# A 2D DFT with a cosine layer behind it: four small moves of work beside a full TensorE

## Chip, cores and metric

The kernel runs on one core of a Trainium2 chip. The metric is the device time of one execution in microseconds (us), lower is better. Every number below is the median of several executions, is read from one profiled execution, or is worked out from such numbers. All executions in this study are recorded as fast (an execution in a slower state would not have been compared).

TensorE multiplies matrices. In this kernel its products go to PSUM, and what the engines read otherwise lies in SBUF (two on-chip memories).

The profile splits TensorE into PE (the matmul passes) and PEld (the weight loads, which overlap the passes: in the kernel before 1932.9 and 1649.2 us of busy time in a span of 1982.3). DVE is VectorE, ACT is ScalarE, POOL is GpSimd, SP is SyncE, which here only issues DMA. A trailing q (SPq) marks an engine's sequencer, which issues its instructions. The granted clock is the share of full speed that TensorE was given (1.00 is full). L276 is line 276 of the kernel; `pB<-G,WT` is an instruction that writes tile pB from tiles G and WT. Nearly every operation goes through a one-line helper, so a line number names the kind of operation, and the tiles tell which one it is.

## The reference, cut to what matters

```python
# x: [8, 3008, 256] float32; w_in: [256, 2048]; w_out: [2048, 256]
X = np.fft.fft(np.fft.fft(x, axis=1), axis=2).real    # over the sequence, then over the channels
X = X.reshape(8 * 3008, 256)
h = X @ w_in
g = h * np.cos(h)
out = g @ w_out                                       # [24064, 256]
```

## The kernel before

The channel DFT is folded into `w_in` at the start (`fold_sin`, `fold_cos` give Ws and Wc). The sequence DFT of a batch uses its symmetries: rows of `x` are added and subtracted ("folds", on GpSimd after the first batch), and the folded rows are multiplied by sine and cosine matrices. Some rows are needed in reversed order; GpSimd fetches these with indirect DMA ("gathers"). Channel 128 is not covered by the folded weights and is computed for all batches at once, early ("ext" in the code).

The rest is 376 equal steps. Eight steps make one tile of 256 columns and its mirror image, so there are 47 tiles. A step makes two hidden blocks (`H`), takes the cosine on ScalarE, multiplies on VectorE, forms four sums on GpSimd (`sum_1` to `sum_4`), and multiplies into four accumulators in PSUM, `pA` to `pD`. Only one set of the four exists, so the next tile's products wait until the old ones have been read. This is how work is placed: each function has a time in units of the planned step `T` = 4.8 us, and the program order of each engine follows from these times.

```python
        for dt, fn in (
            (-1.9, ext), (0.0, mm_P), (0.9, dbl), (2.17, mm_Q), (3.55, h_minus),
            ...
            (T + 0.9, r_minus), (T + 1.5, sin_plus), (T + 2.2, g_plus), (T + 2.21, sin_minus),
            (T + 2.9, g_minus), (T + 2.91, sum_1), (T + 3.6, sum_3), (T + 4.4, sum_2),
            (2 * T + 0.3, sum_4), (2 * T + 0.87, mm_X1), (2 * T + 3.04, mm_X2),
        ):
            at(t + dt, lambda fn=fn, i=i: fn(i))
```

At the end of a tile its accumulators are combined. Five operations read them: a ScalarE copy of half of pA and four VectorE adds, the last of which is `comb_3`:

```python
    def comb_3(q):
        T = tiles[q]
        vtt(T.v, T.v, T.acc[3], ALU.add)           # VectorE; acc[3] is pD
    ...
            turns = ((T + 1.2, comb_3), (2 * T + 1.0, turn_u), (3 * T + 1.0, turn_v))
        for dt, fn in ((1.45, comb_copy), (4.2, comb_1), (T + 1.0, comb_2), (T + 1.1, comb_22)) + turns:
```

The DFT of channel 128 reads it with rows on partitions (`MC,xe 128*8` in the timelines below). Before, it was loaded with batches on partitions and then turned through DRAM:

```python
    def turn_ext():
        rows, xs = state["rows"], state["xs"]
        for g in range(2):
            spin(out=xe_dr[g], in_=rows[g][:, 0:768])              # to DRAM
            spin(out=xr_dr[g], in_=rows[g][:, 247::-1])
        for g in range(2):
            spin(out=xs[:, g, :, 0:4], in_=...)                    # back, in runs of a few rows
            ...                                                    # (three more loads for each g)
```

The loads and gathers of batch `b` start 8 steps ahead of the point `s0` where its period of 47 steps begins, one gather a step, and the folds start one step ahead of `s0`:

```python
        l0 = s0 - (8 if b > 1 else 1.2)
        ...
                at((l0 + n) * T + 1.3, lambda b=b, n=n: gather_x(b, state["L"], n))
        f0 = max(7, s0 - 1)
        f1 = s0 + 38
```

## Time and profile before

| | before |
|---|---|
| median, lowest and highest of 3 runs | 1984.32, 1982.59 to 1985.54 us |
| span of the profiled run | 1982.3 us |
| PE busy | 1932.9 us (98%) |
| other engines busy | 72 to 73% each |

The head of the page, the packet count and the chain of work that ended last, of the kernel before:

```profile
PE 1932.9 (98%) x8858; PEld 1649.2 (83%) x8858; DVE 1425.2 (72%) x2386; ACT 1454.8 (73%) x2807; POOL 1418.9 (72%) x1947
...
DMA packets 283624, 65.85 MB, mean 33 GB/s; under 512 B 264570, under 2 KB 275458, under 8 KB 283474
...
PE 84%; DVE 5%; POOL 4%; ACT 3%; issue 2%; SPq 1%; DMA 1%; DVEq 0%; POOLq 0%
```

TensorE bounds this kernel: the other engines matter only where they make it wait. The table by windows of the kernel before says where it was idle; its columns are the window, its length, and the busy time (with instruction count) of each engine, then the granted TensorE clock, the DMA share and GB/s:

```profile
0.00:50.00 50.00, 39.84 (x121) 21.93 (x122) 26.25 (x59) 14.17 (x27) 35.77 (x55) 0.97 1.07 255
50.00:100.00 50.00, 49.34 (x223) 40.91 (x222) 36.27 (x60) 37.12 (x71) 45.09 (x73) 1.00 1.29 36
100.00:150.00 50.00, 25.56 (x126) 19.29 (x125) 17.56 (x29) 18.04 (x36) 18.99 (x31) 0.76 0.36 22
150.00:400.00 250.00, 247.99 (x1138) 213.20 (x1139) 185.21 (x312) 188.86 (x365) 191.46 (x259) 1.00 0.14 31
```

Half of the window from 100 to 150 us is idle. The timeline of PE and that of SP, kernel before (start, duration, instruction, and in brackets the idle time before it and what ended it):

```profile
106.01 0.59 PE L276 MATMUL pD<-G,w 128*128 128x256 f32 x2
130.26 3.73 PE L276 MATMUL H<-MC,xe 128*8 128x190 f32 x28 [23.66 <-POOL xe L285]
```

```profile
67.20 0.42 SPq L162 DMA_DIRECT2D xe_dr<-x  x1
...
77.01 39.34 SPq L162 DMA_DIRECT2D xs<-xe_dr  x3
...
123.53 1.04 SPq L162 DMA_DIRECT2D xs<-xr_dr  x1
```

This is "the hole": TensorE stood still for 23.66 us because the round trip of channel 128 through DRAM, whose first store was issued at 67.20 us, had not come back. The three loads at 77.01 us alone held SyncE's sequencer for 39.34 us.

The table of waits of the kernel before (engine and line, what it waited for: total us, how often, longest):

```profile
PEld H L276 <- POOL xe L285: 24.4, 2, 24.1
...
PE H L276 <- POOL xe L285: 23.7, 1, 23.7
...
PEld pB L276 <- POOL G L285: 18.5, 49, 1.0
...
PE pB L276 <- POOL G L285: 2.3, 8, 0.6
```

The hole stands in it twice, once for the weight load and once for the matmul. The third and fourth lines are one wait too, that of the product into pB for a GpSimd sum.

### The profile page before, as it was taken

How to read it: one execution, taken by the hardware profiler on the slowest of the kernel's cores; microseconds unless marked ns; L12 is line 12 of the kernel's file. 1: busy time of each engine (PE TensorE's matmuls, PEld its weight loads, DVE VectorE, ACT ScalarE, POOL GpSimd, SP SyncE). 2: the span in 40 equal slices, each digit the busy share in tenths (PEclk: the TensorE clock that was granted, in tenths of full speed). 3: DMA queues.
4: the chain of work that ended last, by engine and by line, in shares of the span. 5: the costliest groups of instructions: out<-in, count | busy, mean ns of one | idle time of the engine just before them, and what ended most of it. 6: DMA issues, size and time to landing. Idle time of an engine off the chain costs nothing.

```text
span 1982.3 us, 28384 instructions
## 1 busy us (share of the span) xinstructions
PE 1932.9 (98%) x8858; PEld 1649.2 (83%) x8858; DVE 1425.2 (72%) x2386; ACT 1454.8 (73%) x2807; POOL 1418.9 (72%) x1947
## 2 busy tenths in 40 slices
PE   7959999999999999999999999999999999999998
PEld 4838888888888888888888888888888888887887
DVE  5737777777777777777767777777776777777777
ACT  2737777777777777777777777777777777777776
POOL 7837768777687767877777776877768786555664
PEclk9979999999999999999999999999999999999999
DMA  9930111102110021100210002111021110100101
GB/s 258 36 22 20 51 32 31 25 12 52 39 22 20 12 60 44 20 11 14 65 45 13 14 13 66 35 19 24 9 67 28 21 21 15 17 11 12 22 11 22
DMA packets 283624, 65.85 MB, mean 33 GB/s; under 512 B 264570, under 2 KB 275458, under 8 KB 283474
## 3 DMA queue, kind: packets, MB, share of 16 engines
q1 hardware_dynamic: 276386, 51.06, 16.2%
q0 software_dynamic: 4912, 12.73, 2.4%
q8 instruction: 70, 1.15, 0.3%
q14 instruction: 80, 0.66, 0.1%
q10 hardware_dynamic: 2176, 0.26, 0.1%
HBM read 39.13 MB, written 24.82 MB: 32 GB/s over the span
## 4 chain that ended last, share of the span: by engine, by line
PE 84%; DVE 5%; POOL 4%; ACT 3%; issue 2%; SPq 1%; DMA 1%; DVEq 0%; POOLq 0%
PE H L276 33%; PE pB L276 14%; PE pC L276 14%; PE pD L276 14%; PE pA L276 7%; POOL G L285 2%; DVE G L790 2%; ACT G L288 1%; SPq L162 1%; POOL xl L152 1%; DVE G L282 1%; POOL e L341 1%; DVE v L282 1%; DVE M L282 1%; ACT E L288 1%
## 5 line engine op out<-in xcount | busy, mean ns | idle before, releaser
L285 POOL TENSOR_TENSOR G<-G 128x256 f32<-128x256 f32 x1500 | 1079.0, 730 | 504.5 <-DVE G L790 416.3
L790 DVE SCALAR_TENSOR_TENSOR G<-H,G 128x512 f32<-128x512 f32 x376 | 256.9, 683 | 289.5 <-ACT G L288 289.0
L282 DVE TENSOR_TENSOR G<-H,G 128x512 f32<-128x512 f32 x376 | 259.8, 691 | 220.9 <-ACT G L288 217.8
L288 ACT ACTIVATE G<-H 128x512 int32<-128x512 f32 x376 | 224.5, 597 | 235.4 <-DVE G L282 234.0
L276 PE MATMUL pC<-G,WT 128*128 128x256 f32 x1504 | 387.4, 379 | 2.7 <-DVE u L282 2.2
L276 PE MATMUL H<-Rr,Wc 128*128 128x256 f32 x1504 | 387.6, 380 | 1.6 <-ACT H L288 0.9
L276 PE MATMUL H<-Ir,Ws 127*128 127x256 f32 x1504 | 387.4, 379 | 0.7 <-ACT E L288 0.7
L288 ACT ACTIVATE E<-H 128x512 f32<-128x512 f32 x376 | 224.2, 596 | 219.0 <-PE H L276 213.9
L288 ACT ACTIVATE H<-Rb,wex 128x256 f32<-128x256 f32 x752 | 360.3, 479 | 26.3 <-DVE G L790 10.3
L276 PEld LDWEIGHTS H<-Rr,Wc 128*128 128x128 f32 x1504 | 283.4, 190 | 50.8 <-ACT H L288 5.4
L276 PEld LDWEIGHTS pC<-G,WT 128*128 128x128 f32 x1504 | 283.8, 189 | 46.8 <-PE H L276 6.8
L276 PEld LDWEIGHTS H<-Ir,Ws 127*128 127x128 f32 x1504 | 282.5, 189 | 44.8 <-ACT E L288 5.9
L288 ACT ACTIVATE G<-G,halfpi 128x512 f32<-128x512 f32 x376 | 269.6, 717 | 1.5 <-DVE G L282 1.5
L282 DVE TENSOR_TENSOR M<-G,M 128x512 f32<-128x512 f32 x376 | 257.7, 685 | 0.0
L282 DVE TENSOR_TENSOR G<-E,H 128x512 f32<-128x512 f32 x376 | 255.1, 678 | 3.1 <-PE H L276 2.7
L790 DVE SCALAR_TENSOR_TENSOR G<-G,M 128x512 f32<-128x512 f32 x376 | 254.1, 676 | 0.4 <-ACT M L288 0.3
L288 ACT ACTIVATE M<-M,halfpi 128x512 f32<-128x512 f32 x376 | 246.6, 656 | 0.4 <-DVE M L282 0.3
L276 PE MATMUL pB<-G,WT 128*128 128x256 f32 x752 | 228.6, 386 | 2.8 <-POOL G L285 2.3
L276 PE MATMUL pB<-G,w 128*128 128x256 f32 x752 | 223.7, 379 | 0.6 <-DVE u L282 0.6
L288 ACT ACTIVATE M<-G 128x512 int32<-128x512 f32 x376 | 224.1, 596 | 0.0
L276 PE MATMUL pA<-G,w 128*128 128x256 f32 x752 | 223.8, 379 | 0.1
L276 PE MATMUL pD<-G,w 128*128 128x256 f32 x752 | 223.7, 379 | 0.0
(150 smaller groups left out, 1855.7 us busy)
## 6 DMA issues: line engine op xcount, KB each, us to landing
out_dram<-ot SPq DMA_DIRECT2D x496, 32.0 KB
xl<-in_x_dram SPq DMA_DIRECT2D x32, 256.0 KB
out_dram<-ot SPq DMA_DIRECT2D x256, 2.0 KB
xl<-in_x_dram SPq DMA_DIRECT2D x31, 128.0 KB
Rb<-r SPq DMA_DIRECT2D x10, 376.0 KB
w<-in_moe_w_in_dram SPq DMA_DIRECT2D x4, 512.0 KB
w<-in_moe_w_out_dram SPq DMA_DIRECT2D x1, 2048.0 KB
MC<-dft_mats SPq DMA_DIRECT2D x2, 942.0 KB
```

Source lines behind the costliest of these rows:

```text
L152: nc.gpsimd.indirect_dma_start(out=L[j][:, part[0] * ND : part[1] * ND], out_offset=None, in_=xflat, in_offset=bass.IndirectOffsetOnAxis(a ...
L162: pin(nc.sync.dma_start(**kw))
L276: nc.tensor.matmul(out_, lhsT=lhsT, rhs=rhs, start=start, stop=stop, skip_group_check=True)
L282: pin(nc.vector.tensor_tensor(out=o, in0=a, in1=b, op=op))
L285: pin(nc.gpsimd.tensor_tensor(out=o, in0=a, in1=b, op=op))
L288: pin(nc.scalar.activation(out=o, in_=i, func=func, **kw))
L341: pin(eng.tensor_tensor(out=o, in0=a, in1=b, op=f))
L790: nc.vector.scalar_tensor_tensor(out=o, in0=h, scalar=TWO_PI, in1=c, op0=ALU.mult, op1=ALU.mult)
```

## The change

It has four parts.

1. **The turn.** Channel 128 is turned by TensorE: slices of the loaded rows are the weights, a small 0/1/-1 matrix (`pick`) is streamed, and the product is the turned and folded channel. The store and loads through DRAM go, and so does the GpSimd fold.
2. **The gathers.** Two adjacent ones are merged, and the loads start 10 steps ahead of `s0`, the folds at `s0`, so that gathers and folds of a batch no longer fall into the same steps.
3. **The copy.** ScalarE copies pD, the last quarter of the product sums, to SBUF. VectorE's add of it moves by nearly a step; the transposes move by a step.
4. **The start.** The last two folds of `w_in` come earlier (one ahead of I's first DFT, the other into another PSUM bank), and the first step's elementwise work goes ahead of an unfold.

The diff, cut to its core (constants, the index table and the first load's bookkeeping are left out):

```diff
+    def open_ext():
+        ps = state["turned"] = bank("H")
+        pin(nc.vector.memset(ps[:, 0:128], 0.0))
+        rows = state["rows"]
+        pin(nc.gpsimd.tensor_copy(out=rows[:, 1024:1148], in_=rows[:, 247::-2]))
     def turn_ext():
-        ... (four stores to DRAM, eight loads back)
+        rows, ps = state["rows"], state["turned"]
+        even, both, less = (pick[0:32, a:z] for a, z in ((32, 40), (32, 48), (48, 56)))
+        d, m = rows[:, 1024:1148], rows[:, 505:761:2]
+        for lhsT, o, rhs in (
+            (rows[:, 0:512:4], C0, both),
+            (rows[:, 2:512:4], C2, both),
+            ... (eight more)
+        ):
+            mm(ps[0 : lhsT.shape[1], o * 16 : o * 16 + rhs.shape[1]], lhsT, rhs, False)
     def fold_ext():
-        ... (six GpSimd operations)
+        xe = spool.tile([128, 8, 2, NB], FP, tag="xe", bufs=1, name="xe")
+        act(xe.rearrange("p m k b -> p (m k b)"), state["turned"][:, 0:128])
...
-    at(-T, turn_ext)
-    e0 = 12 * T
-    at(e0 + 1.35, fold_ext)
+    e0 = 10 * T
+    at(e0 - 2 * T + 2.905, open_ext)
+    at(e0 - 2 * T + 4.75, turn_ext)
+    at(e0 - T + 1.46, fold_ext)
...
+    def comb_copy3(q):
+        T = tiles[q]
+        T.p3 = spool.tile([128, 512], FP, tag="p3", bufs=1, name="p3")
+        act(T.p3, T.acc[3])
     def comb_3(q):
-        vtt(T.v, T.v, T.acc[3], ALU.add)
+        vtt(T.v, T.v, T.p3, ALU.add)
-            turns = ((T + 1.2, comb_3), (2 * T + 1.0, turn_u), (3 * T + 1.0, turn_v))
+            turns = (
+                (T + 2.3, comb_copy3),
+                (2 * T + 1.0, comb_3),
+                (3 * T + 1.0, turn_u),
+                (4 * T + 1.0, turn_v),
+            )
...
+            if j == 2 or b < NB - 1:
+                yield j, (3, 6), n                 # gathers: one of (3,6) for (3,4) and (5,6)
...
-        l0 = s0 - (8 if b > 1 else 1.2)
+        l0 = s0 - (10 if b > 1 else 1.2)
-        f0 = max(7, s0 - 1)
-        f1 = s0 + 38
+        f0 = max(7, s0)
+        f1 = s0 + (36 if b > 1 else 38)
...
+    fold_cos(3)                                    # now ahead of I_even.first
...
+    ahead = {r_minus: T + 0.3, sin_plus: T + 0.85, sin_minus: T + 0.86,
+             g_plus: T + 0.92, g_minus: T + 0.93, sum_1: T + 0.94}
+            if i == 0:
+                dt = ahead.get(fn, dt)
-        (0.95, lambda: fold_sin(3, "pD")),
+        (0.95, lambda: fold_sin(3)),
-        (3.0, lambda: state.update(wc3=fold_mms(3, 0, "pA"))),
-        (4.81, lambda: act(Wc[:, 1536:2048], state.pop("wc3"))),
```

More of the change, by code (lines that the diff above doesn't have):

```diff
@@ L85, in _pick_consts @@
 def _pick_consts():
-    m = np.zeros((128, 32), np.float32)
+    m = np.zeros((128, 56), np.float32)
     m[np.arange(128), np.arange(128) % 32] = 1.0
+    q = np.arange(32)
+    c = 32 + q % 16 // 2
+    m[q, c] = 1.0
+    m[q, c + 8] = np.where(q // 16 == q % 2, 1.0, -1.0)
+    m[q, c + 16] = -1.0
     return m
@@ L95, in _row_consts @@
     for base in (HALF, SEQ):
-        cols += [base - _row_of(m) for m in (C0, C2, M1, X1)]
-    cols.append(SEQ - _row_of(D1))
+        cols += [base - _row_of(m) for m in (C2, M1, X1)]
+    cols += [SEQ - _row_of(m) for m in (C0, D1)]
     return np.clip(np.stack(cols, axis=1), 0, SEQ - 1).astype(np.uint32)
@@ L144, with gather_x @@
     xflat = x.rearrange("b s d -> (b s) d")
-    ix = cpool.tile([128, 11], U32, tag="ix")
+    ix = cpool.tile([128, 10], U32, tag="ix")
     nc.sync.dma_start(out=ix, in_=IX_dr.ap())
-    def gather_x(b, L, n):
-        j, part = GATHERS[n]
+    def gather_x(b, L, g):
+        j, part, n = g
         pin(
@@ L162, in spin, with gathers, load_x @@
         pin(nc.sync.dma_start(**kw))
-    GATHERS = [(0, (D1, D1 + 1)), (3, (D1, D1 + 1))] + [
-        (j, part) for j in (2, 1) for part in ((5, 6), (3, 4), (1, 3), (0, 1))
-    ] + [(1, (4, 5))]
-    def n_gathers(b):
-        return len(GATHERS) - (b < NB - 1)
-    def load_x(b, gather=True):
+    def gathers(b):
+        yield 0, (1, 2), 0
+        yield 3, (1, 2), 1
+        for j, n in ((2, 2), (1, 5)):
+            if j == 2 or b < NB - 1:
+                yield j, (3, 6), n
+            else:
+                yield j, (3, 4), n
+                yield j, (5, 6), 8
+                yield j, (4, 5), 9
+            yield j, (1, 3), n + 1
+            yield j, (0, 1), n + 2
+    def load_x(b):
         L = [
@@ L176, in load_x @@
         ]
-        if gather:
-            for n in range(n_gathers(b)):
-                gather_x(b, L, n)
-        def load(out, in_):
-            pin(nc.sync.dma_start(out=out, in_=in_))
         for j, row in ((0, 0), (3, HALF)):
-            load(
-                L[j].rearrange("p (m d) -> p m d", d=ND)[:, C0 : C2 + 1 : 2],
-                bass.AP(
+            spin(
+                out=L[j].rearrange("p (m d) -> p m d", d=ND)[:, C0 : C2 + 1 : 2],
+                in_=bass.AP(
                     tensor=xt,
@@ L192, in load_x, with load_d @@
             )
-            load(L[j][:, Y * ND : X1 * ND], xrows(b, row + 504, 2, 128, 2))
-            load(L[j][:, X1 * ND :], xrows(b, row + 249, 2, 128, 1))
-        for j, row in ((2, HALF), (1, SEQ)):
-            if b < NB - 1 or j == 2:
-                load(L[j][:, 4 * ND : 5 * ND], xrows(b, row - 247, 2, 128, 1))
-        return L
+            spin(out=L[j][:, Y * ND : X1 * ND], in_=xrows(b, row + 504, 2, 128, 2))
+            spin(out=L[j][:, X1 * ND :], in_=xrows(b, row + 249, 2, 128, 1))
+        return L
+    def load_d(b, L, j):
+        if b < NB - 1 or j == 2:
+            row = SEQ if j == 1 else HALF
+            spin(out=L[j][:, 4 * ND : 5 * ND], in_=xrows(b, row - 247, 2, 128, 1))
     CC = cpool.tile([128, 512], FP, tag="CC")
@@ L219 @@
     L_first = load_x(0)
+    for g in gathers(0):
+        gather_x(0, L_first, g)
+    load_d(0, L_first, 2)
     load_w1(1)
+    load_d(0, L_first, 1)
     def w1_cols(h, c0, c1):
@@ L254 @@
     Rx4 = cpool.tile([128, 32], FP, tag="Rx4")
-    pick = cpool.tile([128, 32], FP, tag="pick")
+    pick = cpool.tile([128, 56], FP, tag="pick")
     nc.gpsimd.memset(R4, 0.0)
@@ L261 @@
     r128_dr = dpool.tile([NB, HALF], FP, tag="r128", name="r128")
-    xe_dr = dpool.tile([2, 2 * NB, 768], FP, tag="xe", name="xe_dr")
-    xr_dr = dpool.tile([2, 2 * NB, 248], FP, tag="xr", name="xr_dr")
     PF = [cpool.tile([128, 128], FP, tag=f"pf{i}", name=f"pf{i}") for i in range(2)]
@@ L596, in load_ext @@
         x1 = spool.tile([128, HALF + 1], FP, tag="rx", bufs=1, name="x1")
-        xs = spool.tile([128, 2, 2 * NB, 8], FP, tag="xs", bufs=1, name="xs")
-        pin(nc.gpsimd.memset(xs, 0.0))
         rows = [x1[0 : 2 * NB], x1[2 * NB : 4 * NB]]
-        state["rows"], state["xs"] = rows, xs
+        state["rows"] = x1[0 : 4 * NB]
         def copy(out, row, ap):
@@ L606, in copy @@
             )
-        with nc.allow_non_contiguous_dma(reason="one channel, then runs of rows"):
+        with nc.allow_non_contiguous_dma(reason="one channel"):
             copy(rows[1][:, 0:1], HALF, [[SEQ * ND, NB], [-HALF * ND, 2], [1, 1]])
@@ L611, in load_ext @@
             copy(rows[1][:, 1:768], HALF - 1, [[HALF * ND, 2 * NB], [-ND, 767], [1, 1]])
-    def turn_ext():
-        rows, xs = state["rows"], state["xs"]
-        with nc.allow_non_contiguous_dma(reason="runs of rows"):
-            for g in range(2):
-                spin(out=xe_dr[g], in_=rows[g][:, 0:768])
-                spin(out=xr_dr[g], in_=rows[g][:, 247::-1])
-            for g in range(2):
-                d = xe_dr[g]
-                spin(
-                    out=xs[:, g, :, 0:4],
-                    in_=d[:, 0:512].rearrange("b (p m) -> p b m", m=4),
-                )
-                spin(
-                    out=xs[:, g, :, 4:6],
-                    in_=d[:, 504:760].rearrange("b (p m) -> p b m", m=2),
-                )
-                spin(
-                    out=xs[:, g, :, 6:7],
-                    in_=d[:, 249:505].rearrange("b (p m) -> p b m", m=2)[:, :, 0:1],
-                )
-                spin(
-                    out=xs[0:124, g, :, 7:8],
-                    in_=xr_dr[g].rearrange("b (p m) -> p b m", m=2)[:, :, 0:1],
-                )
@@ L638, in fold_ext @@
-    def fold_ext():
-        xs = state["xs"].rearrange("p g (b h) m -> p g b h m", h=2)
-        xe = spool.tile([128, 2, NB, 8], FP, tag="xe", bufs=1, name="xe")
-        a, b = xs[:, 0, :, 0], xs[:, 1, :, 0]
-        gtt(a, a, xs[:, 1, :, 1], ALU.add)
-        gtt(b, b, xs[:, 0, :, 1], ALU.add)
-        gtt(xe[:, 0], a, b, ALU.add)
-        gtt(xe[:, 1], a, b, ALU.subtract)
-        d, m = xe[:, 0, :, 7], xe[:, 0, :, 5]
-        gtt(xe[:, 0, :, 1], d, m, ALU.add)
-        gtt(m, d, m, ALU.subtract)
+    def open_ext():
[3 more added lines that the diff above has]
+        pin(nc.gpsimd.tensor_copy(out=rows[:, 1024:1148], in_=rows[:, 247::-2]))
@@ new lines, in turn_ext @@
+    def turn_ext():
+        rows, ps = state["rows"], state["turned"]
[4 more added lines that the diff above has]
+            (rows[:, 2:512:4], C2, both),
+            (rows[:, 504:760:2], Y, both),
+            (rows[:, 249:505:2], X1, both),
+            (d, D1, both),
+            (m, M1, both),
+            (d, 6, even),
+            (m, 6, even),
+            (d, 7, even),
+            (m, 7, less),
+        ):
+            mm(ps[0 : lhsT.shape[1], o * 16 : o * 16 + rhs.shape[1]], lhsT, rhs, False)
@@ L665, in dft_ext @@
                         ps[32 * g : 32 * g + NB, o : o + rhs.shape[1]],
-                        xe[:, kodd, :, (0, 7, 2, 4, 5, 6, 1)[m]],
+                        xe[:, 7 if m == M1 and not kodd else m, kodd],
                         rhs,
@@ L1001, in mid_pick @@
         po = state["mo"] = bank("H")
-        mm(po[0:32, 0:ND], pick, state["mh"][:, 0:ND], True)
+        mm(po[0:32, 0:ND], pick[:, 0:32], state["mh"][:, 0:ND], True)
     def mid_store():
@@ L1072 @@
     T = PERIOD
+    ahead = {
+        r_minus: T + 0.3,
+        sin_plus: T + 0.85,
+        sin_minus: T + 0.86,
+        g_plus: T + 0.92,
+        g_minus: T + 0.93,
+        sum_1: T + 0.94,
+    }
     for i in range(total):
@@ L1181 @@
         s0 = (b - 1) * steps_b
-        l0 = s0 - (8 if b > 1 else 1.2)
-        at(l0 * T + 0.1, lambda b=b: state.update(L=load_x(b, b == 1)))
-        if b > 1:
-            for n in range(n_gathers(b)):
-                at(
-                    (l0 + n) * T + 1.3,
-                    lambda b=b, n=n: gather_x(b, state["L"], n),
-                )
-        f0 = max(7, s0 - 1)
-        f1 = s0 + 38
+        l0 = s0 - (10 if b > 1 else 1.2)
+        at(l0 * T + 0.1, lambda b=b: state.update(L=load_x(b)))
+        for n, g in enumerate(gathers(b)):
+            t = l0 * T + (n * T + 1.3 if b > 1 else 0.11)
+            at(t, lambda b=b, g=g: gather_x(b, state["L"], g))
+        for j in (2, 1):
+            at(t + 0.01, lambda b=b, j=j: load_d(b, state["L"], j))
+        f0 = max(7, s0)
+        f1 = s0 + (36 if b > 1 else 38)
         at(f0 * T, lambda b=b: begin_folds(b))
```

## The prediction

> **What bounds the kernel now.** The busy table gives TensorE 1932.9 of 1982.3 us (98%), the other engines 72 to 74%; the chain of waits is 84% TensorE. In the timeline a 256-column matmul (two passes) starts every 0.43 us[...]. So only TensorE's idle time and added work count. The table by windows shows its 49 us of idleness: 10 in the first 50 us, 24.4 between 100 and 150 us, some 7 in steady work, 6 in the tail.
>
> **The hole, 106.6 to 130.3 us.** The waits there are TensorE <- GpSimd xe <- DMA. Channel 128 goes to DRAM and back in short runs: first store issued at 67.2 us, last xs load at 123.5; the xe matmuls start at 130.26 after 23.66 us of idleness. The granted clock was 0.5 from 109.3 to 133.2, so these 28 passes (3.73 us) also ran cold. [...] The change keeps the element-wise loads of x1 (landed by 67.2 us, when the dependent store went) and drops all behind them. The turn stands behind step 8 (about 83 us), so it should not wait: -23.7 us, and -1.4 of cold clock.
>
> **Added on TensorE:** 10 small matmuls, 20 passes of 8 or 16 columns, bound by weight loads. Estimate from 133 ns per xe pass and 190 ns per 128-column load: +3 us. Copies and a memset elsewhere are off the path.
>
> **Start.** fold_cos(3) fills the 1.55 us gap before 32.81 us; fold_sin(3) loses the 1.80 us wait for pD at 38.80. First-step elementwise work goes ahead of R_odd's unfold; GpSimd, which paces steps 3 to 8 (4.77 us each), starts earlier. Two gathers fewer (1.25 us each) precede the fold that waited 3.8 us for a gather until 21.37: 1 to 2 us more. Together -5.5 us (3 to 7).
>
> **Steady state.** Gathers of later batches now end before the folds begin; before, a gather and a fold in one step cost TensorE 0.2 to 0.4 us (pB after GpSimd's G, near 319, 324, 555, 560 us and so on): -4 us. ScalarE's copy of pD (46 of about 0.6 us) takes a PSUM read from VectorE at the busy tile boundary, but frees pD later, with some 0.8 us to spare: 0 to +1 us.
>
> **Sum.** 1984.3 - 25.1 + 3 - 5.5 - 4 + 0.5 = about 1953 us, range 1947 to 1960. That is 1.6%: within 2% 0.92, faster by over 2% 0.06, slower 0.02.
>
> **What would show it right.** No TensorE gap over 2 us after 30 us; clock 1.0 from about 27 us to the tail; xe passes under 3 us in sum; the 20 pick passes 2 to 5 us in sum; step 3 begins 4 to 7 us before 57.8; steady windows show the same TensorE work with waits on GpSimd sums near zero; GpSimd gathers 66 instead of 81; about 24,000 fewer packets under 512 B.
>
> **What would make it wrong.** The turn waits for x1, a PSUM bank or the GpSimd copy: a new hole. The later pD makes TensorE wait at each of 47 tiles (0.5 us each would cost 20). The second load of slot 4 waits for the gather into it and blocks the DMA queue behind it: matrices come late at the start. Upside: first gathers land over 2 us earlier.

## The result

The kernel after took 1941.71 us (median of 4 runs, 1939.79 to 1942.69), beside 1984.93 us (4 runs, 1982.59 to 1985.73) for the kernel before in the same rounds. The ratio is 0.9783 (95% interval 0.9766 to 0.9800): faster by 2.2%. A ratio here is always the mean time of one kernel's fast runs over that of the other's of the same rounds, so it is not quite the ratio of the quoted medians. The prediction was 1953 us with a range from 1947 to 1960 and 0.92 on "within 2%": the time lies below the range, and the class is another.

The same parts of the page, kernel after:

```profile
PE 1921.9 (99%) x8878; PEld 1657.6 (85%) x8878; DVE 1426.7 (74%) x2387; ACT 1478.6 (76%) x2854; POOL 1412.0 (73%) x1926
...
DMA packets 258994, 67.59 MB, mean 35 GB/s; under 512 B 239970, under 2 KB 250858, under 8 KB 258842
...
PE 95%; DVE 2%; ACT 1%; issue 1%; DMA 1%; POOL 0%; SPq 0%; DVEq 0%; POOLq 0%
```

GpSimd (4% before, 0% after) and VectorE (5% and 2%) have nearly left the chain that ended last. The table by windows, kernel after:

```profile
0.00:50.00 50.00, 42.73 (x132) 23.23 (x133) 28.65 (x64) 15.85 (x30) 34.44 (x56) 0.97 1.09 266
50.00:100.00 50.00, 50.00 (x257) 42.64 (x256) 33.86 (x55) 35.95 (x69) 41.81 (x69) 1.00 0.58 34
100.00:150.00 50.00, 48.58 (x220) 40.93 (x219) 40.94 (x69) 39.56 (x76) 40.05 (x54) 1.00 0.17 32
150.00:400.00 250.00, 249.96 (x1160) 218.52 (x1159) 185.66 (x310) 195.66 (x379) 193.26 (x261) 1.00 0.15 32
```

The hole is gone. The timeline of PE, kernel after, shows what stands in its place, the 20 passes of the turn and the 28 of the channel's DFT:

```profile
82.84 2.93 PE L284 MATMUL H<-pick,x 32*128 32x16 f32 x20
...
95.46 2.08 PE L284 MATMUL H<-MC,xe 128*8 128x190 f32 x28
```

And the wait for GpSimd's sums, in the table of waits of the kernel after:

```profile
PEld pB L284 <- POOL G L293: 1.9, 3, 1.0
```

### Where the 42.4 us came from

Busy time is a poor ruler for a TensorE that is nearly always busy, so the traces were cut by the program's own clock: every step has one ScalarE instruction `E<-H`, and its start in the timeline of ACT dates the step. Times between these marks, in us:

| kernel | start to step 0 | 0 to 8 | 8 to 20 | 20 to 375 | 375 to end |
|---|---|---|---|---|---|
| before | 37.04 | 46.26 | 88.90 | 1793.31 | 16.82 |
| after | 37.51 | 41.55 | 65.09 | 1778.74 | 17.02 |
| gained | -0.47 | 4.71 | 23.81 | 14.57 | -0.20 |

The gains sum to 42.42 us, the difference of the two profiled spans (1982.3 and 1939.9 us). The prediction had 22.1 us net for the hole, 5.5 for the start and 3.5 for the steady steps. The first two are near. The steady steps gave 14.6, four times as much, and this is where the prediction went wrong.

It is worth seeing how little of this the busy time shows. The windows from 150 to 1900 us, kernel before and then kernel after:

```profile
150.00:1900.00 1750.00, 1742.52 (x8047) 1501.99 (x8048) 1284.17 (x2138) 1329.81 (x2571) 1275.80 (x1729) 1.00 0.13 28
```

```profile
150.00:1900.00 1750.00, 1747.57 (x8123) 1522.48 (x8122) 1294.81 (x2151) 1364.56 (x2639) 1278.49 (x1725) 1.00 0.13 29
```

PE seems idle for 7.5 us before and 2.4 us after, 5 us apart; yet in the same 1750 us it did 76 passes more, 0.9%. The end of a matmul is modelled in this profile, and short waits can vanish into it: the 18.5 us that the weight loads into pB waited for GpSimd's sums in the kernel before stand as 2.3 us at the matmuls. Between these two traces the weight loads tell more: their busy time rose by 20.5 us (1.4%), the matmul busy time by 5.1 us (0.3%).

### The profile page after: what moved, and what is told of

Same layout as the page of the kernel before. It is cut to its first block, busy times and chain, and to the rows that moved or that the text cites. A ratio compares the mean times of both kernels' runs of the same rounds, so it can differ in the third digit from the quotient of the medians.

```text
span 1939.9 us, 28429 instructions
## 1 busy us (share of the span) xinstructions
PE 1921.9 (99%) x8878; PEld 1657.6 (85%) x8878; DVE 1426.7 (74%) x2387; ACT 1478.6 (76%) x2854; POOL 1412.0 (73%) x1926
## 4 chain that ended last, share of the span: by engine, by line
PE 95%; DVE 2%; ACT 1%; issue 1%; DMA 1%; POOL 0%; SPq 0%; DVEq 0%; POOLq 0%
PE H L284 38%; PE pC L284 17%; PE pD L284 16%; PE pB L284 16%; PE pA L284 8%; DMA w<-in_moe_w_in_dram 1%; DVE G L787 1%; ACT G L296 1%; DVE G L290 0%; ACT E L296 0%; DVE M L290 0%; DVE v L290 0%; DVE ab L290 0%; DVE ot L900 0%; DVE u L290 0%
## 5 line engine op out<-in xcount | busy, mean ns | idle before, releaser
L284 PEld LDWEIGHTS H<-Ir,Ws 127*128 127x128 f32 x1504 | 284.7, 189 | 41.9 <-ACT E L296 1.4
L284 PE MATMUL pB<-G,WT 128*128 128x256 f32 x752 | 224.0, 379 | 1.0 <-POOL G L293 1.0
L284 PE MATMUL pD<-G,WT 128*128 128x256 f32 x752 | 223.8, 379 | 0.0
```

The lines of the kernel that those rows point to most:

```text
L284: nc.tensor.matmul(out_, lhsT=lhsT, rhs=rhs, start=start, stop=stop, skip_group_check=True)
```

## The experiments

### Theories

For the 14.6 us of steady steps there are two candidates: part 2 (gathers ahead of the folds) and part 3 (the copy). The prediction gave part 2 4 us and part 3 nothing or a small loss.

- **Theory A, the tile boundary.** At the end of each tile VectorE is so loaded by four adds that its products, then GpSimd's sums, then TensorE come late. Taking one add away from that spot is what gains.
- **Rival B, the gathers.** The weight-load waits for GpSimd's sums come from gathers that delay those sums, and the copy is neutral, as predicted.
- **Within A:** the gain comes from *moving* the add (A1), or from the add reading SBUF in place of PSUM and so getting shorter (A2).

The evidence for A in the two traces is the timeline of DVE around one tile boundary. Before:

```profile
365.49 0.68 DVE L282 TENSOR_TENSOR u<-p,pB 128x512 f32<-128x512 f32 x1
...
367.44 0.68 DVE L282 TENSOR_TENSOR v<-u,pC 128x512 f32<-128x512 f32 x1
368.15 0.42 DVE L282 TENSOR_TENSOR u<-v,pC 128x256 f32<-128x256 f32 x1
368.68 0.69 DVE L282 TENSOR_TENSOR v<-v,pD 128x512 f32<-128x512 f32 x1
...
369.88 0.68 DVE L790 SCALAR_TENSOR_TENSOR G<-G,M 128x512 f32<-128x512 f32 x1
```

After, around a boundary of the same kind:

```profile
335.08 0.68 DVE L290 TENSOR_TENSOR u<-p,pB 128x512 f32<-128x512 f32 x1
...
337.03 0.68 DVE L290 TENSOR_TENSOR v<-u,pC 128x512 f32<-128x512 f32 x1
337.75 0.42 DVE L290 TENSOR_TENSOR u<-v,pC 128x256 f32<-128x256 f32 x1
...
338.69 0.68 DVE L787 SCALAR_TENSOR_TENSOR G<-G,M 128x512 f32<-128x512 f32 x1
...
341.83 0.69 DVE L290 TENSOR_TENSOR v<-v,p 128x512 f32<-128x512 f32 x1
```

The last add (`v<-v,...`) stood before two products; the second of these (`G<-G,M`, g_minus) releases GpSimd's sums. Counted from the first add, g_minus starts after 4.39 us before and 3.61 us after. GpSimd and PE follow it. The timeline of POOL, before and then after:

```profile
370.11 3.04 POOL L285 TENSOR_TENSOR G<-G 128x256 f32<-128x256 f32 x4 [1.59 <-DVE G L790]
```

```profile
338.91 3.03 POOL L293 TENSOR_TENSOR G<-G 128x256 f32<-128x256 f32 x4 [0.80 <-DVE G L787]
```

GpSimd waited 1.59 us for g_minus before and 0.80 us after. The timeline of PE, before:

```profile
370.62 1.03 PE L276 MATMUL H<-Rr,Wc 128*128 128x256 f32 x4
...
372.39 0.70 PE L276 MATMUL pB<-G,WT 128*128 128x256 f32 x2
372.92 1.05 PE L276 MATMUL H<-Ir,Ws 127*128 127x256 f32 x4
```

PE, after:

```profile
340.21 1.03 PE L284 MATMUL H<-Rr,Wc 128*128 128x256 f32 x4
...
341.94 0.59 PE L284 MATMUL pB<-G,WT 128*128 128x256 f32 x2
342.37 1.03 PE L284 MATMUL H<-Ir,Ws 127*128 127x256 f32 x4
```

From the step's first H product to its last it is 2.30 us before and 2.16 us after, and PE's line shows no idle time in either: the wait is in the weight load and in a pass that looks a little longer (0.70 in place of 0.59 us). The marks of the steps (`E<-H`) show the same. Before, two steps at a boundary lasted 5.276 and 4.403 us; after, all of these are 4.752 us. The long step is not wholly made good by the short one: 5.276 + 4.403 - 2 x 4.752 = 0.175 us a tile are lost, and 46 of them are about 8 us.

Each experiment below is read by the same marks; all gave correct results. The whole table:

| kernel | ratio to before (95%) | to step 0 | 0 to 8 | 8 to 20 | 20 to 375 |
|---|---|---|---|---|---|
| after | 0.9783 (0.9766 to 0.9800) | 37.51 | 41.55 | 65.09 | 1778.74 |
| e1_undo_copy | 0.9817 (0.9804 to 0.9830) | 36.39 | 41.58 | 68.50 | 1788.30 |
| e2_only_copy | 0.9959 (0.9943 to 0.9974) | 38.03 | 45.43 | 94.77 | 1784.73 |
| e3_move_no_copy | 0.9963 (0.9948 to 0.9978) | 36.73 | 41.58 | 68.42 | 1815.36 |
| e4_copy_no_move | 0.9832 (0.9817 to 0.9847) | 37.34 | 41.56 | 66.89 | 1789.77 |
| e5_old_gathers | 0.9795 (0.9781 to 0.9808) | 36.06 | 41.55 | 66.71 | 1784.72 |
| e5c_single_new_times | 0.9757 (0.9740 to 0.9773) | 36.57 | 41.56 | 66.71 | 1778.75 |
| e6_undo_turn | 0.9927 (0.9910 to 0.9944) | 35.47 | 41.56 | 98.78 | 1778.75 |
| e7_undo_start | 0.9791 (0.9779 to 0.9803) | 36.31 | 46.22 | 65.38 | 1778.75 |
| e9_only_turn | 0.9870 (0.9855 to 0.9885) | 36.50 | 46.19 | 66.00 | 1793.08 |
| b1_all_and_more | 0.9777 (0.9761 to 0.9793) | 42.20 | 42.19 | 62.70 | 1778.85 |
| c1_after_again | 0.9784 (0.9771 to 0.9798) | 36.62 | 41.56 | 66.71 | 1778.78 |
| b2_turn_in_two | 0.9773 (0.9759 to 0.9786) | 36.43 | 41.55 | 62.93 | 1778.81 |

Each row is one trace. The steady stretch repeats to within 0.11 us over the seven traces that have the code of after in it (0.23 us between before and e9), so there the marks separate what the ratios alone would leave open.

### The copy: undone, and alone

Undone, from the kernel after:

```diff
     def comb_3(q):
-        vtt(T.v, T.v, T.p3, ALU.add)
+        vtt(T.v, T.v, T.acc[3], ALU.add)
-            turns = ((T + 2.3, comb_copy3), (2 * T + 1.0, comb_3), (3 * T + 1.0, turn_u), (4 * T + 1.0, turn_v))
+            turns = ((T + 1.2, comb_3), (2 * T + 1.0, turn_u), (3 * T + 1.0, turn_v))
```

> The kernel after the change, but the last quarter of the product sums is again added by VectorE straight from PSUM, in the step and order of before (no ScalarE copy). Theory A (the burst of four VectorE adds at each tile boundary delays the activation products, then GpSimd's sums, then TensorE's pB by a net 0.17 us per tile, 46 tiles): about 8 us slower than the kernel after, 1949.7 us, and every third step of a tile lasts 5.28 us and the next 4.40 us, as before. Theory B (the copy is worth nothing, as I predicted, and all the extra steady gain is the gathers'): 1941.7 us, no such steps.

Alone, from the kernel before, it is the same edit the other way round, with the tile xs laid into free columns of x1:

```diff
-        xs = spool.tile([128, 2, 2 * NB, 8], FP, tag="xs", bufs=1, name="xs")
+        xs = x1[:, 1024:1280].rearrange("p (g b m) -> p g b m", g=2, m=8)
+    ... comb_copy3, comb_3 and turns as in the kernel after
```

> The kernel before with only this part of the change: ScalarE copies the last quarter, VectorE adds it one step later, the transposes one step later. (The channel-128 scratch tile xs is laid into free columns of x1[...].) Theory A: 8 us faster than the kernel before, about 1977 us; the 5.28/4.40 us pair of steps is gone, while the hole of 24 us stays. Theory B: 1984 to 1985 us.

Measured: e1 took 1951.18 us (5 runs, 1950.75 to 1953.49), e2 1980.79 (6 runs, 1974.71 to 1982.86), before 1987.78 (11 runs, 1984.07 to 1990.27) beside both. In the steady stretch undoing the copy cost 9.6 us, and doing it alone gained 1793.31 - 1784.73 = 8.6 us. The pair of uneven steps came back in e1 (5.281 and 4.402 us) and was gone in e2. The weight-load waits for GpSimd's sums, e1 and then e2:

```profile
PEld pB L284 <- POOL G L293: 10.6, 32, 1.0
```

```profile
PEld pB L276 <- POOL G L285: 10.6, 21, 1.0
```

They were 18.5 us with 49 waits before and 1.9 us with 3 after; each of the two parts takes away part of them, and the place tells which: of e1's 32 waits 29 lie behind a tile's end, as 29 did before; of e2's 21 only one does, and after has none there. Rival B falls in the form "only the gathers". e2's total is not a clean measure of the copy: its hole was longer (8 to 20 took 94.77 us, before 88.90). TensorE ran dry at the same time (106.6 us), but the last load of the round trip was issued at 128.91 us in place of 123.53; why the loads came later is not shown.

### Is it the copy or the move?

e4 keeps the copy and puts the add back at its old place. e3 moves the add behind g_minus but lets it read pD in PSUM.

```diff
 e4, from the kernel after:
-                (T + 2.3, comb_copy3), (2 * T + 1.0, comb_3), (3 * T + 1.0, turn_u), (4 * T + 1.0, turn_v),
+                (T + 1.05, comb_copy3), (T + 1.2, comb_3), (2 * T + 1.0, turn_u), (3 * T + 1.0, turn_v),
 e3, from the kernel after:
-        vtt(T.v, T.v, T.p3, ALU.add)
+        vtt(T.v, T.v, T.acc[3], ALU.add)
-                (T + 2.3, comb_copy3), (2 * T + 1.0, comb_3),
+                (T + 2.95, comb_3),
```

> The kernel after with the ScalarE copy of pD, but VectorE adds it at the old place, behind u, v, u in the same burst, and the transposes at their old steps. Theory A: the burst is as long as before (the add took 0.69 us from PSUM and takes 0.69 us from SBUF), so the 5.28/4.40 us pair of steps is back and it is 8 us slower than the kernel after, up to 12 as ScalarE's copy stands ahead of the sines. Rival D (what helps is that VectorE no longer reads PSUM, or that pD comes free from ScalarE): as the kernel after, within 2 us.

> The kernel after, but VectorE adds the last quarter straight from PSUM, just behind the activation products (g_minus) of the same step: the add is moved out of the burst, without the ScalarE copy. Theory A: the burst is as short as in the kernel after, but pD comes free about 0.7 us after TensorE wants it (g_minus ends at about 339.4 us in the trace after, the add 0.6 us later, TensorE starts pD at 339.35): about 0.7 us per tile, 30 us in all, near 1972 us, with TensorE waiting for VectorE v before pD. Rival C (the order on VectorE is all that matters, the copy is only decoration): as the kernel after, within 2 us.

Measured: e4 1954.36 us (4 runs, 1953.22 to 1954.69), e3 1980.53 (4 runs, 1978.94 to 1981.07), before 1987.83 (12 runs) beside them. With the copy but without the move, the whole gain is lost (11.0 us in the steady stretch; the steps at the boundary are 5.283 and 4.403 us again). A2 falls: the source of the add made no difference to its length, 0.69 us from PSUM and 0.69 us from SBUF in the lines above (medians 687 and 685 ns).

The transposes (`turn_u`, `turn_v`, on VectorE) move with the add in e1, e2 and e4, and no run moves one without the other. In the timeline of the kernel before, the first of them starts at 373.02 us, behind the product into pB at 372.39, so at that boundary they are not what delayed it; this is read from one trace and not tested.

With the move but without the copy, it is far worse: the steady stretch took 1815.36 us, 36.6 us more than after. The table of waits of PE in e3 names the reason:

```profile
PE pD L284 <- DVE v L290: 26.4, 46, 1.0
```

The products of the next tile into pD now wait for the late add, once at each of the 46 boundaries; that step lasts 5.527 us, and 46 x (5.527 - 4.752) = 35.7 us (about 30 were expected). So the two halves belong together. The add is worth moving because VectorE (74% busy in the kernel after) has time for it a step later; the copy (46 of 0.6 us), which ScalarE (76% busy) fits in, is what frees pD in time so that it can be moved. A1 stands, with that condition.

### The gathers

e5 takes the old times and the single gathers back; e5c the single gathers only, with the new times.

```diff
 e5 and e5c, from the kernel after:
+        if b > 1:
+            ... one gather each of (5, 6) and (3, 4) in place of (3, 6)
 e5 alone:
-        l0 = s0 - (10 if b > 1 else 1.2)
+        l0 = s0 - (8 if b > 1 else 1.2)
-        f0 = max(7, s0)
-        f1 = s0 + (36 if b > 1 else 38)
+        f0 = max(7, s0 - 1)
+        f1 = s0 + 38
```

> The kernel after, with the gathers of batches 2 to 7 single and timed as before, and the folds over the 39 steps of before (batches 0 and 1 unchanged). Theory A: 14.6 us of steady gain less 8.0 of the copy leave 6.6; the start of each batch's folds shows 4.5 us of it, so 5 to 6.6 us slower than the kernel after: about 1947.5 us, with TensorE waiting on GpSimd sums in the first three steps of the folds. Theory B: 13 to 14 us slower, about 1955 us.

> The kernel after, but the gathers of batches 2 to 7 are single again (nine or ten instead of eight, the neighbouring rows not merged), at the new times: one per step from ten steps before the folds, all ahead of them; folds over the 36 new steps. If the 6.0 us of the gather part come from keeping gathers and folds out of the same step, steps 20 to 375 take 1778.8 us as after (within 1 us). If they come from the merging (fewer GpSimd issues), 1784.7 us as with the old gathers.

Measured: e5 1946.94 us (5 runs, 1945.21 to 1948.92), beside before at 1987.78; e5c 1941.06 (4 runs, 1940.08 to 1942.21), beside before at 1988.4 (7 runs). The ratio of e5 (0.9795) alone would not separate it from after (0.9783), since the intervals overlap. The marks do: 20 to 375 took 5.98 us more in e5. All of it lies where gathers and folds met: in the first five steps of the batches' periods (steps 20 to 330) e5 spent 153.27 us and after 147.30 us. e5c is equal to after (1778.75 and 1778.74 us), so the later folds and earlier loads count and the merging of gathers does not. That the 8.58 us of e2 and the 5.98 us of e5 sum to 14.56 of the 14.57 us proves nothing more: in the steady stretch e2 and e5 are the same program (1784.73 and 1784.72 us), one reached by adding the copy and one by taking the gathers away. The gathers alone, before against e1, gave 1793.31 - 1788.30 = 5.0 us, so the two parts alone sum to 13.6 us and together give 1.0 us more. The copy is worth 8.6 to 9.6 us and the gathers 5.0 to 6.0, by which comes first.

### The turn: undone, and alone

e6 is the kernel after with the old turn through DRAM at 12 T; e9 is the kernel before with the new turn only.

```diff
 e6, from the kernel after (e9, from the kernel before, is the reverse):
-    e0 = 10 * T
-    at(e0 - 2 * T + 2.905, open_ext)
-    at(e0 - 2 * T + 4.75, turn_ext)
-    at(e0 - T + 1.46, fold_ext)
+    at(-T, turn_ext)
+    e0 = 12 * T
+    at(e0 + 1.35, fold_ext)
     ... turn_ext and fold_ext as in the kernel before (in e6 xs lies in free columns of x1)
```

> The kernel after, with channel 128 turned through DRAM at the old steps (xs in free columns of x1). The prediction's sizes: 25.1 us of hole and cold clock back, 3 us of small matmuls gone: 22 us slower, 1964 us. By the step times of the two traces (26.6 us and 2.8 us): 24 us slower, 1965.5 us. A hole of 23 to 28 us before the xe matmuls, clock 0.5 in it. If the hole came from something else that the change also moved (the loads of batch 1, say), it stays under 10 us.

> The kernel before with only the turn of channel 128 by TensorE (loads as before, the turn behind step 8, the DFT of it at step 10). The hole goes, 2.8 us of small matmuls come: 24 us faster than the kernel before, more if the hole is longer on this chip (30 us were seen in one run): ratio 0.985 to 0.989. The steady steps stay those of the kernel before, with the 5.28/4.40 us pair.

Measured: e6 1973.57 us (6 runs, 1967.44 to 1977.2), e9 1961.06 (4 runs, 1960.08 to 1962.64). From step 8 to 20, e9 took 66.00 us against 88.90 in before, a gain of 22.9 us; e6 took 98.78 against 65.09. The steady stretch does not notice the turn (e6 as after, e9 within 0.23 us of before), so the turn's gain is that of the hole and nothing else. e6 lost more than e9 gained because its hole was longer: the step with the hole (12 to 13) took 32.3 us in before, 38.4 in e2 and 41.9 in e6, and e6 was 32 us slower than after where 22 to 24 were expected. The traces say where its extra time comes from. In before, TensorE was idle from 106.60 to 130.26 us; in e6 from 100.54 to 134.16. It ran dry 6.1 us earlier, because with the new start it reached step 8 at 77.03 us in place of 83.30, and the round trip ended 3.9 us later. Step 20 came at 175.8 us in e6 and at 172.2 in before. So as long as the hole stands, a faster start only makes TensorE wait sooner; the start pays only together with the turn. Why the round trip ended later in e6 and e2 is not shown: both have xs in x1, but I did not test whether that is the reason, and the runs of e6 spread over 10 us.

### The start

```diff
 e7, from the kernel after: the folds of w_in and the first step's order as before
-    fold_cos(3)
-            if i == 0:
-                dt = ahead.get(fn, dt)
-        (0.95, lambda: fold_sin(3)),
+        (0.95, lambda: fold_sin(3, "pD")),
+        (3.0, lambda: state.update(wc3=fold_mms(3, 0, "pA"))),
+        (4.81, lambda: act(Wc[:, 1536:2048], state.pop("wc3"))),
```

> The kernel after with the start of before in what concerns order: fold_sin(3) through bank pD, fold_cos(3) through pA at step 0, the first step's sines and products behind R_odd's unfold (first gathers as after). From the first E to the ninth, 46.26 us before and 41.55 us after: 4.7 us slower than the kernel after, all of it before step 8. The prediction had 3.5 to 4 us for this part.

Measured: 1945.86 us (6 runs, 1944.62 to 1946.77). Steps 0 to 8 took 46.22 us, as in before (46.26), in place of 41.55: 4.7 us. I did not divide this between the two folds and the first step's order. The time to step 0 is another matter. It lay between 35.5 and 38.0 us in traces whose loads and gathers at the start are the same or nearly so, so the effect of the merged first gathers, and of the second half of `w_in` being issued at 12.93 us in place of 9.13, can't be read from it.

### A try at more

The table shows one more loss: 8 to 20 took 65.1 us in after but 66.7 in e5c, which is the same code there. In e5c's trace the granted clock fell to 0.5 for 3.4 us right after the turn. That was so in six of nine traces with the 20 passes in one go (not in after, e7 and e9; in e1 it was 6.8 us). Two kernels tried to do better. b1 does the turn in 12 passes (six products, wider `pick`), spreads the 8-partition adds of channel 128 over steps with room, shifts the first tile's transposes by two steps, and reorders the loads and the folds of `w_in` at the start. b2 is the same without the changes at the start, and with the turn cut in two, dense products between the halves:

```diff
 b2, from the kernel after:
-    at(e0 - 2 * T + 4.75, turn_ext)
+    at(e0 - 2 * T + 4.75, lambda: turn_ext(0))
+    at(e0 - T + 0.86, lambda: turn_ext(1))
-    at(e0 + 2 * T + 1.0, lambda: ext_rows(1, vtt))
-    at(e0 + 5 * T + 1.0, lambda: ext_rows(0, vtt))
+    at(e0 + 2 * T + 1.0, lambda: ext_unfold(1))
+    at(e0 + 3 * T + 1.0, lambda: ext_plus(1))
+    ... (and four more, to e0 + 13 * T)
-                (3 * T + 1.0, turn_u),
-                (4 * T + 1.0, turn_v),
+                ((3 if q else 5) * T + 1.0, turn_u),
+                ((4 if q else 6) * T + 1.0, turn_v),
 b1, besides the 12 passes and the spread adds:
+    load_w1(0)                     # a second time, right behind the first
-    load_w1(1)                     # second half of w_in: now behind the first DFT matrix
-    fold_sin(2)                    # now behind the first DFTs
-    fold_cos(2)
```

> A try to beat both, on the kernel after: (1) the loads and gathers of batch 0 and the first DFT matrix go ahead of the second half of w_in, the first gathers single so that no load waits for one of them, ten filler matmuls; folds 2 and 3 of w_in moved behind the first DFTs; (2) the 10 turning matmuls merged to 6; (3) the eight-partition adds of channel 128 spread over free steps, tile 0's transposes two steps later. Expected from the trace after: start 2 to 3 us, turn 1.1 us (12 passes for 20 of 0.14 us), the 2.6 us that steps 12 to 16 take beyond 4.752 us each: 5 to 6.5 us faster than the kernel after. If the start is held by the DMA and not by the order of its loads, only 3 us.

> The kernel after itself, on the chip and beside the runs of the other experiments: 0.9783 of the kernel before on the first chip, 0.976 to 0.979 here. [...] the granted clock is 0.5 for 3.4 us behind them (so in five of eight earlier traces with this turn) and steps 8 to 20 take about 66.8 us in place of 65.1.

> The kernel after, its start unchanged, with (1) the turn as 6 matmuls in place of 10, three behind step 8 and three behind the next step's first product, so that dense matmuls stand between them; (2) the eight-partition adds of channel 128 spread over free steps and tile 0's transposes two steps later. No drop of the clock between 30 us and the tail; steps 8 to 20 take 62 to 63 us: 2.4 us faster than the kernel after, 4 us where that one's clock drops. If the drop does not come from the thin turn but from chance, it shows here too.

Measured: b1 took 1944.76 us (4 runs, 1944.33 to 1945.31), 3 us more than after. It gained 2.4 us between step 8 and 20, and lost 4.7 us before step 0 (42.20 us) and 0.6 from there to step 8. But its edit has `load_w1(0)` twice, by a slip as it seems, for what was expected of b1 does not speak of it. So the first half of `w_in` was loaded two times, and the products read the second copy. The timeline of SP, after and then b1:

```profile
1.63 0.93 SPq L167 DMA_DIRECT2D w<-in_moe_w_in_dram  x2
```

```profile
1.64 2.05 SPq L167 DMA_DIRECT2D w<-in_moe_w_in_dram  x4
```

TensorE began with `w_in` at 11.00 us in place of 7.55, after 4.73 us of waiting for this load, and the first fold of x started at 16.6 us in place of 14.07. So b1 does not say whether the new order of the loads is good or bad: the second copy and the new order were not separated.

b2 took 1938.64 us (5 runs, 1938.42 to 1940.12), beside 1940.76 (5 runs, 1940.38 to 1943.58) for the kernel after and 1984.31 (9 runs, 1981.52 to 1986.84) for before in the same rounds. It is 2.1 us faster than after; the ranges of the runs do not overlap, though the intervals of the two ratios do. It beats both kernels, and by little. Part of the gain lies where the adds were spread: step 12 to 13 took 5.09 us in b1 and b2, and 6.7 in after and c1. The PE timelines of c1 (which is the kernel after) and of b2 show the turn:

```profile
81.96 2.92 PE L284 MATMUL H<-pick,x 32*128 32x16 f32 x20
```

```profile
81.76 1.34 PE L283 MATMUL H<-pick,x 32*128 32x16 f32 x6
83.03 1.13 PE L283 MATMUL H<-Rr,Wc 128*128 128x256 f32 x4
84.09 0.87 PE L283 MATMUL H<-pick,x 32*128 32x16 f32 x6
```

And the window just behind it, in c1 and then in b2 (the clock is the third number from the end):

```profile
86.00:90.00 4.00, 4.00 (x13) 3.25 (x12) 1.39 (x3) 3.18 (x7) 1.04 (x2) 0.61 0.00 0
```

```profile
86.00:90.00 4.00, 4.00 (x21) 3.50 (x20) 3.14 (x6) 3.34 (x9) 2.21 (x4) 1.00 0.00 0
```

At the lower clock (0.61 on average in this window) PE did 13 passes in these 4 us, at the full one 21, and both count as 100% busy. In c1 the granted clock was 1.00 from 61 to 85 us and 0.50 from 85.7 to 89.1 us, right behind the turn. What lowers it behind the turn in six of the nine traces and not in the other three is not shown: the 20 passes took 2.92 us in e5c, which has the drop, and 2.93 in after, which has none, with no idle gap of PE around them in either. b2 has no drop, with its passes in two stretches of 1.34 and 0.87 us; but b1, whose 12 passes go in one stretch of 2.0 us, has none either. So fewer passes may be enough, and that the cut is what helps b2 is not shown.

## Why the prediction was wrong, point by point

The prediction's sum of gains was 31.1 us, the measured one 42.4, 11.3 more.

- **What bounds the kernel:** right. TensorE is the chain, and every gain was a wait of TensorE taken away.
- **The hole ("-23.7 us, and -1.4 of cold clock", "+3 us" for the turn):** right. Net 22.1 us were predicted; 23.8 were measured, and 22.9 with the turn alone. The turn took 2.93 us for 20 passes (expected 2 to 5), the channel's own passes 2.08 us (under 3; before 3.73, at a granted clock of 0.50), and the packets under 512 B fell by 24,600 (about 24,000). In the trace of after the weight loads were busy for 2.84 of the turn's 2.93 us, and the spacing of its passes followed the weights, not the 8 or 16 streamed columns: about 118 ns for 128 weight columns and 108 ns for 124, with steps of one or two elements, but 233 ns for the first four passes, whose slices take every fourth element. Whether the step or the place at the front makes these four slow was not tested.
- **The start ("-5.5 (3 to 7)"):** right in size, 4.7 us from the order and 0.5 us lost before step 0, the latter within the noise of that stretch. Step 3 came 3.9 us earlier, just under the 4 to 7 foretold. The "1 to 2 us more" from fewer gathers did not show.
- **The gathers ("-4 us"):** right mechanism, too small. They gave 6.0 us.
- **The copy ("0 to +1 us"): this is the step that failed.** It was entered as a loss of 0.5 us and gained 8.6 (alone; 9.6 on top of the gathers), which is 9.1 of the 11.3 us. The prediction saw that the copy "takes a PSUM read from VectorE at the busy tile boundary", and then looked only at the side that could get worse, the moment when pD comes free. It did not follow the other side: that the add moves out from in front of g_minus, which GpSimd's sums and through them TensorE wait for. The profile had shown that side, but not where it was looked for: PE's own idle time there was small (2.3 us with 8 waits), while the weight-load row for the same product had 18.5 us with 49 waits, 29 of them (8.7 us) behind a tile's end. The prediction ascribed the waits of pB for GpSimd's G that it saw to gathers and folds alone ("near 319, 324, 555, 560 us and so on").
- **What it said would show it right** held, but for step 3 (above): after 30 us no gap of TensorE exceeds 1.3 us, the clock is 1.0 from 22.8 us to the tail, and the gathers are 66 in place of 81. These signs test the hole and the gathers; none of them tested what the copy is worth.
- **What it said could go wrong:** the risk at pD was real, since without the copy each of 46 tiles lost 0.8 us (e3); with the copy the slack it had estimated sufficed. The DMA queue was held up at the start as it feared (it waited 1.2 us for a gather, and the second half of `w_in` was issued at 12.93 us in place of 9.13), with no effect on the time that could be read.

So the 11.3 us are, with the copy counted first: 9.1 from the copy, 2.0 from the gathers, 1.7 from the hole, less 1.3 at the start and 0.2 at the end.

Still open: why the round trip through DRAM ended 4 to 6 us later in e6 and e2 than in before; what the change at the start does to the time of step 0; why the granted clock fell behind the turn in six of nine traces and not in the other three.

## What to carry to other kernels

When one engine is full, look for its waits in the row that starts first (here the weight loads) and by counting steps in the trace, not in its busy share: 18.5 us of waits showed as 2.3 us of matmul idle time. Then place each wait in the program before explaining it: the 49 waits were two causes mixed, and it was the 29 behind a tile's end that pointed to the copy. At such a place ask what the loaded helper engine does just ahead of the operation that the full engine waits for, and move out what can wait; a cheap copy on an engine with room that frees the buffer early may be what makes the move possible. Measured in the steady stretch against e1, which has neither: both together gained 9.6 us, the move alone lost 27.1, the copy alone lost 1.5. And look at the parts of a change together: in e6 the faster start brought nothing, because the hole behind it stood.
